# Part of the first expert's work moved into the routing of the last batch, and the router in half batches

## The chip, the cores and the metric

The kernel runs on one core of a Trainium2 chip. The core has TensorE (matmuls, PE in the profile; PEld is its weight load), VectorE (DVE), ScalarE (ACT), GpSimd (POOL) and SyncE (SP), which run side by side and wait for each other on semaphores, and DMA queues that SP and POOL fill. The metric is the device time of one execution in microseconds (us).

## The reference

In short, attention with a window, then a mixture of eight experts in which each token goes to one expert:

```python
scores = scale * np.matmul(q, k.transpose(0, 1, 3, 2)) + bias     # B 4, H 8, S 768, D 64
scores = np.where(is_global | is_local, scores, -1000000000.0)    # 8 global keys, 96 local
a = softmax(scores); x = (a @ v) -> (B*S, H*D) = (3072, 512)
logits = (x / |x|) @ (expert_emb / |expert_emb|).T / tau           # 8 experts
expert_idx = argmax(logits); gate_w = softmax(logits)[expert_idx]
for e in range(8):
    mask = expert_idx == e
    out[mask] = gate_w[mask, None] * (np.maximum(x[mask] @ w1[e], 0) @ w2[e])   # 512 -> 1024 -> 512
```

By the reference's own arithmetic the experts get 406, 310, 510, 319, 322, 369, 472 and 364 of the 3072 tokens; 315 of expert 0's are in the first three of the four batches.

## The kernel before

Everything is float32. `window_attention` runs 32 steps, four for each of eight groups (a batch has two groups of four heads). A step `s` of group `g` scores two units of 96 to 192 queries (`score`, L395), exponentiates them on ACT (`grow`, L399), multiplies them with a table on DVE (`weigh`, L406), transposes what later groups need (`turn`, L376), and multiplies the step before with v and with ones (`attend`, L421 and L429). After every second `attend` the three PSUM tiles `od` are copied to `xd` (ACT one, DVE two, L434 to L436); there is one set of `od`, so the next `attend` waits for these copies.

When a half batch has been attended to in both groups, its three chunks of 128 tokens are routed one chunk a step: `turn_x` transposes the attention output, `turn_sums` the softmax sums and the product of the chunk before (L456, L458), `store_x` scales a row, sends it to `x_dram` and squares it on ACT (L488), and `score_experts` multiplies with the expert embeddings (L494). `choose`, a generator in three parts, then finds the expert (DVE), ranks each token among those of its expert with two matmuls (L199 `prefix`, L200 `ones`) and a running count `cnt` (L213, L214, a pair for each chunk), and computes the gate. POOL scatters token number and gate to `meta`, one indirect DMA for each chunk (L228, `meta<-mt,slot`); `meta` has a list of slots for each expert.

The experts follow. `choose_widths` turns the counts into one of 13 widths for each expert, which each engine loads into a register (L836) for a switch. `load_rows` brings an expert's list (`emt<-meta`, on SP, after all scatters), converts it (`ids`, L753) and gathers the rows (`xg<-x_dram,ids`, POOL, four DMAs of 128 rows). `turn_rows` transposes them (L771), `expert` multiplies with `w1` in the width's arm (L809, 64 passes, a float32 matmul being two) and applies relu, and `second` multiplies with `w2`, 16 passes for each 128 slots (L781), scales, and scatters to the output (L785). While an expert computes, rows and weights (2 MB for `w1`, 2 MB for `w2`) of the next are loaded; those of expert 0 come in parts during attention.

PE, DVE, ACT and SP follow the order in which the code issues (`ORDERED`); POOL's order is found by the scheduler. An engine works strictly in its order.

## Time and profile before

| | us |
|---|---|
| median of 3 runs (lowest, highest) | 636.59 (631.88, 640.8) |
| the profiled execution's own time | 636.79 |
| its span in the profile | 634.8 |
| PE busy in the span | 559.0 (88%) |
| DVE busy | 169.8 |
| ACT busy | 141.6 |
| POOL busy | 99.6 |

The span starts with the first instruction that the profiler counts and ends with the last. Busy time is a sum over stages that have different limits, and a matmul that runs at half clock is busy twice as long.

### The profile page before, as it was taken

To read this page: it belongs to the slowest core of one execution; us is meant where nothing else is said; L and a number is where in the kernel's file an instruction comes from. 1 tells how busy PE (TensorE), PEld (TensorE's weight loads), DVE (VectorE), ACT (ScalarE), POOL (GpSimd) and SP (SyncE) were. 2 spreads that over 40 slices of the span, in tenths; PEclk is the share of its full clock that TensorE was granted. 3 is DMA by queue.
4 is the path that set the end of the run, shared out by engine and by line. 5 is a ranking of instruction groups with operands and counts; after the bars stand their busy time and mean duration, and the time that the engine had idled before them with its cause. 6 is when DMAs were issued, how large, how long until landed. Compare 5 with 4: busy or idle time off the path is not lost.

```text
span 634.8 us, 8682 instructions
## 1 busy us (share of the span) xinstructions
PE 559.0 (88%) x3314; PEld 338.6 (53%) x3314; DVE 169.8 (27%) x445; ACT 141.6 (22%) x345; POOL 99.6 (16%) x138
## 2 busy tenths in 40 slices
PE   4999998898596307999999999999999999999990
PEld 3778886686474204554744444655645544545540
DVE  2555667566375701021020020020100110100000
ACT  4866765665252100100100100100101101100100
POOL 2100004004003324001303001303013013011010
PEclk9999998998797556999999999999999999999995
DMA  9999899995002214722644113643346215010000
GB/s 184 214 208 252 212 233 129 65 230 131 34 18 67 36 15 123 265 89 88 217 152 161 68 50 138 218 153 116 119 160 218 101 69 217 2 36 34 1 34 22
DMA packets 109987, 77.40 MB, mean 122 GB/s; under 512 B 90744, under 2 KB 90872, under 8 KB 109826
## 3 DMA queue, kind: packets, MB, share of 16 engines
q1 hardware_dynamic: 100850, 60.16, 39.8%
q0 software_dynamic: 5488, 14.71, 6.4%
q10 hardware_dynamic: 3488, 0.79, 0.6%
q8 instruction: 52, 0.85, 0.6%
q14 instruction: 109, 0.89, 0.5%
HBM read 62.83 MB, written 13.59 MB: 120 GB/s over the span
## 4 chain that ended last, share of the span: by engine, by line
PE 59%; issue 2%; POOL 1%; DMA 1%; DVE 0%; POOLq 0%; DVEq 0%
PE work L781 29%; PE big L809 27%; PE work L771 2%; DMA xg<-x_dram,ids 1%; POOL xg L757 0%; POOL out_dram L785 0%; POOL meta L228 0%; DVE y L784 0%; POOLq L792 0%; DVE ids L753 0%; DVEq L993 0%; DVE flags L851 0%; DVE xT L772 0%; POOLq L757 0%
## 5 line engine op out<-in xcount | busy, mean ns | idle before, releaser
L781 PE MATMUL work<-w2t,hT 128*128 128x512 f32 x432 | 187.4, 594 | 0.0
L809 PE MATMUL big<-xT,w1t 128*128 128x320 f32 (+5 forms) x512 | 173.1, 499 | 2.6 <-issue 2.6
L809 PEld LDWEIGHTS big<-xT,w1t 128*128 128x128 f32 x512 | 97.9, 191 | 77.8 <-issue 45.0
L781 PEld LDWEIGHTS work<-w2t,hT 128*128 128x128 f32 x432 | 81.5, 190 | 101.0 <-issue 99.5
L811 ACT ACTIVATE hT<-big 128x640 f32<-128x640 f32 (+5 forms) x32 | 26.6, 830 | 355.8 <-PE big L809 355.8
L406 DVE TENSOR_TENSOR ex<-ex,table 126x768 f32<-126x768 f32 x64 | 57.9, 904 | 64.2 <-ACT ex L399 59.5
L785 POOL DMA_INDIRECT out_dram<-y,ids x27 | 26.9, 997 | 302.5 <-DVE y L784 230.5
L784 DVE TENSOR_SCALAR y<-work,emt 128x512 f32<-128x512 f32 x27 | 20.3, 751 | 185.2 <-PE work L781 185.2
L772 DVE COPY xT<-work 128x512 f32<-128x512 f32 x32 | 20.2, 685 | 159.3 <-PE work L771 159.3
L399 ACT ACTIVATE ex<-pa 126x384 f32<-126x384 f32 (+1 forms) x128 | 53.6, 476 | 30.3 <-PE pa L395 27.6
L395 PE MATMUL pa<-qT,kT 64*126 64x192 f32 (+1 forms) x512 | 50.6, 336 | 3.4 <-ACT qT L381 3.0
L421 PE MATMUL od<-ex,v 126*64 126x192 f32 (+1 forms) x576 | 47.8, 312 | 4.0 <-DVE xd L435 4.0
L395 PEld LDWEIGHTS pa<-qT,kT 64*126 64x126 f32 x512 | 41.4, 190 | 11.1 <-issue 5.9
L421 PEld LDWEIGHTS od<-ex,v 126*64 126x64 f32 x576 | 35.3, 139 | 12.5 <-DVE xd L435 4.5
L771 PE MATMUL work<-ident,xg 128*128 128x128 f32 x128 | 19.0, 295 | 22.5 <-DMA xg<-x_dram,ids 22.5
L228 POOL DMA_INDIRECT meta<-mt,slot x24 | 26.3, 1094 | 66.9 <-DVE ok L509 21.5
L757 POOL DMA_INDIRECT xg<-x_dram,ids x32 | 30.8, 962 | 25.3 <-issue 19.7
L771 PEld LDWEIGHTS work<-ident,xg 128*128 128x128 f32 x128 | 15.4, 151 | 27.4 <-issue 23.9
L429 PE MATMUL od<-ex,ones 126*32 126x192 f32 (+1 forms) x576 | 27.5, 315 | 0.0
L376 PE MATMUL pa<-ident,q 128*128 128x128 f32 x96 | 17.2, 297 | 7.8 <-ACT lS L497 7.2
L488 ACT ACTIVATE sq<-xs 128x512 f32<-128x512 f32 x24 | 15.1, 631 | 38.5 <-DVE xs L482 34.0
L376 PE MATMUL pa<-ident,k 128*128 128x128 f32 x96 | 17.2, 296 | 6.0 <-DMA k<-in_k_dram 5.5
(118 smaller groups left out, 286.5 us busy)
## 6 DMA issues: line engine op xcount, KB each, us to landing
w1t<-in_moe_w_dram SPq DMA_DIRECT2D x7, 2048.0 KB, 9.6
w2t<-in_moe_w_dram SPq DMA_DIRECT2D x7, 2048.0 KB, 12.5
v<-in_v_dram SPq DMA_DIRECT2D x32, 192.0 KB, 5.4
x_dram<-xs SPq DMA_DIRECT2D x24, 256.0 KB, 2.7
k<-in_k_dram SPq DMA_DIRECT2D x28, 192.0 KB, 4.4
q<-in_q_dram SPq DMA_DIRECT2D x28, 192.0 KB, 4.2
w1t<-in_moe_w_dram SPq DMA_DIRECT2D x4, 512.0 KB
w2t<-in_moe_w_dram SPq DMA_DIRECT2D x4, 512.0 KB, 5.1
```

The lines of the kernel that those rows point to most:

```text
L376: nc.tensor.transpose(ps[:, r * P : (r + 1) * P], src[:, 3 * half + r, :, :], k.ident[:])
L395: nc.tensor.matmul(u.sp[e][0:ROWS, a * n : (a + 1) * n], lhsT=t.kT[rows, j, 0:ROWS], rhs=t.qT[rows, j * BLK : j * BLK + n], start=True, st ...
L399: nc.scalar.activation(u.ex[:, e], u.sp[e][0:ROWS, 0 : 2 * u.n].rearrange("p (a c) -> p a c", a=2), AF.Exp, scale=k.scale)
L406: nc.vector.tensor_tensor(out=exv, in0=exv, in1=tab[:, :, 0 : u.n // BLK, :], op=ALU.mult)
L421: nc.tensor.matmul(g.od[a][e * D : (e + 1) * D, at : at + c1 - c0], lhsT=g.v[0:ROWS, 2 * a + e, u.j, :], rhs=u.ex[:, e, a, c0:c1], start=f ...
L429: nc.tensor.matmul(g.od[2][32 * i : 32 * i + 32, at : at + c1 - c0], lhsT=k.ones[0:ROWS, 0:32], rhs=u.ex[:, e, a, c0:c1], start=first, sto ...
L757: i = nc.gpsimd.indirect_dma_start(out=xg[:], out_offset=None, in_=k.x_dram[:], in_offset=bass.IndirectOffsetOnAxis(ap=ids[:, j : j + 1], ...
L771: k.nc.tensor.transpose(ps[:, c, :], xg[:, c * P : (c + 1) * P], k.ident[:])
L781: nc.tensor.matmul(ps[:], lhsT=hT[:, f, j * P : (j + 1) * P], rhs=w2[:, f, :], start=f == 0, stop=f == k.NF - 1)
L785: nc.gpsimd.indirect_dma_start(out=k.out[:, :], out_offset=bass.IndirectOffsetOnAxis(ap=ids[:, j : j + 1], axis=0), in_=y[:], in_offset=No ...
L809: nc.tensor.matmul(ps[:, i, 0:w], lhsT=w1[:, c, f * P : (f + 1) * P], rhs=xT[:, c, 0:w], start=c == 0, stop=c == k.NC - 1)
L811: nc.scalar.activation(hT[:, 2 * f2 : 2 * f2 + 2, 0:w], ps[:, :, 0:w], AF.Relu)
```

## The change

The softmax sums, products and scores of a half batch (three chunks) are now made at once: `turn_sums` is six matmuls against four columns of the identity in place of six transposes, `score_experts` four matmuls of 384 columns in place of twelve of 128. A half goes through phases 0 to 3, one a step. The router runs once for each of batches 0 and 1, and once for each half of batches 2 and 3. The rank's totals come from one matmul for each chunk that adds to the following chunks, so the loop of pairs on `cnt` is gone; the square root on POOL moves from the first part of `choose` to the second.

In the last batch the order of steps is: first halves of both groups, then second halves. After the third batch is routed (step 28) `first_base` notes how many of expert 0's slots are filled, up to 256, and `first_rows` (end of step 30) fetches the first 256 slots. `first_turn` transposes them ahead of the last `attend`. Their product with `w1` (`first_product`, eight pieces of 8 passes) stands in between and behind the routing of the last half, and their product with `w2` (`second`, twice) ahead of the remaining rows of expert 0, whose list now starts at a slot known at run time (a register of SP). The width of expert 0 is that of the remaining slots. The weights of expert 1 are loaded in the last four steps of attention, where they were loaded behind the rows of expert 1 before. `choose_widths` moves into the ordered part. `meta` has three numbers a slot: the row in `x_dram` (in which a zero row now lies between batches 2 and 3), the row of the output, and the gate. Pools wait tile by tile for the space that they take over.

TensorE, from the ranking of the last half batch on. Before (`lS` is a chunk's scores, `oh` the choice, `pi` the widths):

```order
L458 MATMUL pa<-ident,lS 128x128
L199 MATMUL pa<-oh,prefix 128x24
L200 MATMUL pa<-oh,ones 128x24
L494 MATMUL pa<-xd,enb 32x128 x4
L458 MATMUL pa<-ident,lS 128x128
L199 MATMUL pa<-oh,prefix 128x24
L200 MATMUL pa<-oh,ones 128x24
L836 TENSOR_LOAD pi
```

After (`xd` the attention output, `fxT` the first slots turned, `w1t` weights):

```order
L467 MATMUL pa<-ident,xd 128x4 x6
L477 MATMUL pa<-xd,enb 32x384 x4
L501 MATMUL pa<-ident,xd 128x128 x8
L574 MATMUL pa<-fxT,w1t 128x256 x4
L487 MATMUL pa<-ident,lS 128x128 x3
L574 MATMUL pa<-fxT,w1t 128x256 x4
L200 MATMUL pa<-oh,prefix 128x24
L203 MATMUL pa<-oh,ones 128x24
L203 MATMUL pa<-oh,ones 128x16
L203 MATMUL pa<-oh,ones 128x8
L574 MATMUL pa<-fxT,w1t 128x256 x24
L921 TENSOR_LOAD pi
```

The 64 passes of the first slots' product now stand around and behind the ranking, ahead of the register loads of `pi`.

SyncE, from the last stores of x on. Before (`emt` is the list of an expert's slots):

```order
L160 DMA w2t<-in_moe_w_dram 128x2x512
L486 DMA x_dram<-xs 128x512 x12
L747 DMA emt<-meta 128x4x2 x2
L993 UNCONDITIONAL_BRANCH
L144 DMA w1t<-in_moe_w_dram 128x4x1024
L149 DMA w2t<-in_moe_w_dram 128x8x512
```

After (`si` is the first slot at which the remaining ones start):

```order
L510 DMA x_dram<-xs 128x512 x6
L162 DMA w1t<-in_moe_w_dram 128x1024 x4
L1055 TENSOR_LOAD si
L1055 ISA x2
L510 DMA x_dram<-xs 128x512
L162 DMA w2t<-in_moe_w_dram 128x2x512 x2
L510 DMA x_dram<-xs 128x512
L831 DMA emt<-meta 128x2x3
L162 DMA w2t<-in_moe_w_dram 128x2x512 x2
L510 DMA x_dram<-xs 128x512 x4
L831 ISA
L831 DMA emt<-meta 128x4x3 x3
```

Expert 1's weights moved in eight parts ahead of and around the first list, and the four x stores of the last steps behind it.

GpSimd, from the scatters of the last batches on. Before (`ss` are the square sums):

```order
L228 DMA meta<-mt,slot 24576x2 x6
L182 TENSOR_TENSOR ss<-ss,half 128x3 x2
L226 COPY mt<-tokid 128x3
L228 DMA meta<-mt,slot 24576x2 x6
L757 DMA xg<-x_dram,ids 128x512 x4
```

After (`out_dram` is the kernel's output):

```order
L233 DMA meta<-mt,slot 28672x3 x3
L837 CAST ids<-emt 128x4
L841 DMA xg<-x_dram,ids 128x512 x2
L208 TENSOR_TENSOR ss<-ss,half 128x3
L231 COPY mt<-tok 128x3x2
L233 DMA meta<-mt,slot 28672x3 x3
L208 TENSOR_TENSOR ss<-ss,half 128x3
L233 DMA meta<-mt,slot 28672x3 x3
L921 TENSOR_LOAD pi x8
L841 DMA xg<-x_dram,ids 128x512 x4
L868 DMA out_dram<-y,ids 3072x512
```

The fetch of the first slots stands between the scatters of the third and the fourth batch, ahead of the root for the last batch's first half; eight register loads stand ahead of the gather of the remaining rows.

The core of the diff (the replaced loop over the steps, unused paths and constants are left out):

```diff
+FIRST = 256
...
-    nc.gpsimd.tensor_tensor(out=ss, in0=ss, in1=k.half[:, 0:n], op=ALU.pow)
...
     w = n * E
-    ohf = oh.rearrange("p t e -> p (t e)")
-    nc.tensor.matmul(cp[:, 0:w], lhsT=k.prefix[:], rhs=ohf, start=True, stop=True)
-    nc.tensor.matmul(cp[:, w : 2 * w], lhsT=k.ones[:], rhs=ohf, start=True, stop=True)
...
+    nc.tensor.matmul(cp[:, 0:w], lhsT=k.prefix[:], rhs=oh.rearrange("p t e -> p (t e)"), start=True, stop=True,
+                     skip_group_check=True)
+    for t in range(n):
+        nc.tensor.matmul(cp[:, (t + 1) * E : w + E], lhsT=k.ones[:],
+                         rhs=oh[:, t : t + 1, :].to_broadcast([P, n - t, E]), start=False, stop=True,
+                         skip_group_check=True)
+
+
+    nc.gpsimd.tensor_tensor(out=ss, in0=ss, in1=k.half[:, 0:n], op=ALU.pow)
     nc.vector.tensor_scalar_add(ss, ss, 1e-6)
...
-    both = new([2, n, E], "both")
-    nc.vector.tensor_copy(out=both.rearrange("p i t e -> p (i t e)"), in_=cp[:, 0 : 2 * w])
-    within, total = both[:, 0], both[:, 1]
-    for t in range(n):
-        nc.vector.tensor_tensor(out=within[:, t, :], in0=within[:, t, :], in1=k.cnt[:], op=ALU.add)
-        nc.vector.tensor_tensor(out=k.cnt[:], in0=k.cnt[:], in1=total[:, t, :], op=ALU.add)
+    both = new([n + 1, E], "both")
+    nc.vector.tensor_tensor(out=both, in0=cp[:, 0 : w + E].rearrange("p (t e) -> p t e", e=E),
+                            in1=k.cnt[:].unsqueeze(1).broadcast_to([P, n + 1, E]), op=ALU.add)
+    nc.vector.tensor_copy(out=k.cnt[:], in_=both[:, n, :])
+    within = both[:, 0:n, :]
...
-    nc.vector.scalar_tensor_tensor(out=slot, in0=best, scalar=float(k.N), in1=rank, op0=ALU.mult, op1=ALU.add)
+    nc.vector.scalar_tensor_tensor(out=slot, in0=best, scalar=float(k.SL), in1=rank, op0=ALU.mult, op1=ALU.add)
...
-    mt = new([n, 2], "mt")
-    nc.vector.reciprocal(out=mt[:, :, 1], in_=gate)
-    nc.gpsimd.tensor_copy(out=mt[:, :, 0], in_=k.tokid[:, b * k.NT + i0 : b * k.NT + i0 + n])
+    mt = new([n, 3], "mt")
+    nc.vector.reciprocal(out=mt[:, :, 2], in_=gate)
+    nc.gpsimd.tensor_copy(out=mt[:, :, 0:2], in_=k.tok[:, b * k.NT + i0 : b * k.NT + i0 + n, :])
...
-    def turn_sums(t, i):
-
+    def turn_sums(hf):
+
+        t, h = hf.t, hf.h
+        hf.ps = bank()
+        for c in range(3):
+            for m in range(2):
+                nc.tensor.matmul(hf.ps[:, 384 + (2 * c + m) * 4 : 384 + (2 * c + m + 1) * 4],
+                                 lhsT=t.groups[m].xd[h][:, 2, c * P : (c + 1) * P], rhs=k.ident[:, 0:P:32],
+                                 start=True, stop=True)
+        nc.vector.reciprocal(out=t.rd[:, 3 * h : 3 * h + 3, :],
+                             in_=hf.ps[:, 384:408].rearrange("p (c h) -> p c h", h=H))
+
+    def score_experts(hf, ps):
+
+        t, h = hf.t, hf.h
+        for a in range(4):
+            nc.tensor.matmul(ps[32 * a : 32 * a + 32, 0 : 3 * P], lhsT=k.enb[:, a, :],
+                             rhs=t.groups[a // 2].xd[h][:, a % 2, :], start=True, stop=True)
+        hf.lS = const.tile([P, 3 * P], F32, name="lS", tag="lS")
+        nc.scalar.copy(out=hf.lS[:], in_=ps[:, 0 : 3 * P])
...
+    def turn_products(hf):
+
+        t, h = hf.t, hf.h
...
+        for c in range(3):
+            nc.tensor.transpose(ps[:, c * P : (c + 1) * P], hf.lS[:, c * P : (c + 1) * P], k.ident[:])
+        tmp = const.tile([P, 12, 2, E], F32, name="lh", tag="lh")
...
+    def start_half(t, h):
+        hf = Net()
+        hf.t, hf.h, hf.phase = t, h, 0
+        late = t.b >= B - 2
+        hf.router = choose(k, t.b, 3 * h if late else 0, 3 if late else NT, t.lg, t.ss, rt_p) if late or h else None
+        return hf
...
+    def half_turns(hf):
+
+        t, i = hf.t, 3 * hf.h + hf.phase
+        xp = turn_x(t, i) if hf.phase < 3 else None
+        if hf.phase == 0:
+            turn_sums(hf)
+        elif hf.phase == 1:
+            turn_products(hf)
+        if xp is not None:
+            store_x(t, i, xp)
+        if hf.router:
+            if hf.phase == 1 or hf.phase == 3:
+                next(hf.router)
+            elif hf.phase == 2:
+                hf.router.send(bank())
+        if hf.phase == 3 and hf.h == 1:
+            check_sums(t)
...
+    def first_base():
+        k.base = k.const.tile([P, E], F32, name="base")
+        nc.vector.memset(k.base[:], 0.0)
+        nc.vector.tensor_scalar(out=k.base[:, 0:1], in0=k.cnt[:, 0:1], scalar1=float(FIRST), scalar2=None, op0=ALU.min)
+        k.si = k.const.tile([P, 1], I32, name="si")
+        nc.vector.tensor_copy(out=k.si[:], in_=k.base[:, 0:1])
+
+    def first_rows():
+        k.first = Net()
+        k.first.rows = load_rows(k, k.meta[0:FIRST, :], k.ea, k.ea2, FIRST // P, nc.gpsimd, k.ZR + 1)
+        k.first.xT = k.ea.tile([P, k.NC, FIRST], F32, name="fxT")
+        k.first.hT = k.ea.tile([P, k.NF, FIRST], F32, name="fhT")
+
+    def first_turn():
+        for j, xg in enumerate(k.first.rows[2]):
+            ps = bank()
+            for c in range(k.NC):
+                nc.tensor.transpose(ps[:, c * P : (c + 1) * P], xg[:, c * P : (c + 1) * P], k.ident[:])
+            nc.scalar.copy(out=k.first.xT[:, :, j * P : (j + 1) * P], in_=ps[:].rearrange("p (c n) -> p c n", c=k.NC))
+
+    def first_product(f):
+        if f % 2 == 0:
+            k.first.ps = bank()
+        ps = k.first.ps
+        for c in range(k.NC):
+            nc.tensor.matmul(ps[:, (f % 2) * FIRST : (f % 2 + 1) * FIRST], lhsT=k.w[0][0][:, c, f * P : (f + 1) * P],
+                             rhs=k.first.xT[:, c, :], start=c == 0, stop=c == k.NC - 1)
+        if f % 2:
+            nc.scalar.activation(k.first.hT[:, f - 1 : f + 1, :], ps[:].rearrange("p (i n) -> p i n", i=2), AF.Relu)
...
+    steps = [(g, p) for g in groups[: 2 * B - 2] for p in range(4)]
+    steps += [(g, p) for h in range(2) for g in groups[2 * B - 2 :] for p in (2 * h, 2 * h + 1)]
...
+        if s == len(steps) - 5:
+            early.close()
+            k.w.append(new_weights(k, k.second_weights()))
+        if s >= len(steps) - 4:
+            for i in range(2):
+                load_weights_part(k, 1, k.w[1], 2 * (s - len(steps) + 4) + i)
...
+        if waiting and (s >= 8 * (B - 1) or all(hf.phase >= 3 for hf in active)):
+            active.append(start_half(*waiting.pop(0)))
+        for hf in active:
+            half_turns(hf)
+            if (hf.t.b, hf.h, hf.phase) == (B - 2, 1, 3):
+                first_base()
...
+        if s == len(steps) - 2:
+            first_rows()
+        prev = t
+
+
+    first_turn()
+    for hf in active:
+        half_turns(hf)
+    attend(*steps[-1])
+    hf = start_half(t, 1)
+    xs = [turn_x(t, 3)]
+    turn_sums(hf)
+    score_experts(hf, bank())
+    xs += [turn_x(t, 4), turn_x(t, 5)]
+    store_x(t, 3, xs[0])
+    store_x(t, 4, xs[1])
+    first_product(0)
+    turn_products(hf)
+    next(hf.router)
+    store_x(t, 5, xs[2])
+    first_product(1)
+    hf.router.send(bank())
+    first_product(2)
+    next(hf.router)
+    check_sums(t)
+    for f in range(3, k.NF):
+        first_product(f)
...
+def load_rows(k, slots, gp, xgp, NJ=CAP // P, cast=None, upto=None):
...
+    mt = gp.tile([P, NJ, 3], F32, name="emt", tag="emt")
...
+    ids = gp.tile([P, NJ, 2], I32, name="ids", tag="ids")
+    (cast or nc.vector).tensor_copy(out=ids[:], in_=mt[:, :, 0:2])
...
+        nc.gpsimd.indirect_dma_start(
+            out=xg[:], out_offset=None, in_=k.x_dram[0 : upto or k.N + 1, :],
+            in_offset=bass.IndirectOffsetOnAxis(ap=ids[:, j, 0:1], axis=0),
...
+    k.need = k.const.tile([P, E], F32, name="need")
+    nc.vector.tensor_tensor(out=k.need[:], in0=k.cnt[:], in1=k.base[:], op=ALU.subtract)
...
         def prepare(e):
             t = Net()
             t.width = n.widths[e]
-            t.rows = load_rows(n, n.meta[e * n.N : e * n.N + CAP, :])
-            t.w = n.w[0]
-            if e > 0:
-                t.w = new_weights(n, (wp_a, wp_b)[e % 2])
-                load_weights(n, e, t.w, n.gathers if e == 1 else ())
+            at = e * n.SL
+            if e == 0:
+                at = nc.values_load(n.si[0:1, 0:1], engines=(SP,), min_val=0, max_val=FIRST)
+            t.rows = load_rows(n, n.meta[bass.ds(at, CAP), :], n.gp, n.xgp)
+            if e < 2:
+                t.w = n.w[e]
+            else:
+                t.w = new_weights(n, (wp_a, n.wp_b)[e % 2])
+                load_weights(n, e, t.w)
             return t
 
         with tc.manual_schedule(engines=ORDERED | set(ARMS)):
+            choose_widths(n)
             coming = prepare(0)
+            second(n, n.first.rows, n.first.hT, n.w[0][1], 0)
             hint(n, coming.width)
+            second(n, n.first.rows, n.first.hT, n.w[0][1], 1)
             coming.xT = n.xtp.tile([P, n.NC, CAP], F32, name="xT", tag="xT")
             turn_rows(n, coming.rows, coming.xT)
             for e in range(n.E):

```

## Rows read from the trace of the kernel before

**Rows 1.** The page, share of 40 slices: busy tenths of TensorE (PE).

```profile
PE   4999998898596307999999999999999999999990
```

**Rows 2.** Stretches: from:to in us, length, busy us (count) by engine, PEclk, DMA.

```profile
104.00:106.00 2.00, 2.00 (x24) 0.99 (x24) 1.73 (x3) 0.72 (x2) 1.70 (x2) 0.50 0.19 59
...
200.00:210.00 10.00, 7.53 (x49) 5.29 (x49) 4.62 (x19) 2.62 (x9) 5.68 (x6) 0.50 0.39 75
```

**Rows 3.** Timeline, attention's end to the first expert: start, us, engine, line, operation.

```profile
194.20 0.70 PE L429 MATMUL od<-ex,ones 126*32 126x192 f32 x16
...
211.81 0.48 PE L458 MATMUL pa<-ident,lS 128*128 128x128 f32 x1 [0.88 <-ACT lS L497]
...
220.16 0.18 DVE L225 RECIPROCAL mt<-gate 128x3 f32<-128x3 f32 x1
...
223.63 0.96 POOL L228 DMA_INDIRECT meta<-mt,slot  x1 [0.30 <-issue]
...
232.36 0.94 SPq L747 DMA_DIRECT2D emt<-meta  x2
...
234.42 0.17 DVE L753 CAST ids<-emt 128x4 int32<-128x4 f32 x1 [13.03 <-DMA emt<-meta]
...
238.90 1.09 PE L771 MATMUL work<-ident,xg 128*128 128x128 f32 x4 [21.30 <-DMA xg<-x_dram,ids]
...
243.39 1.08 PE L771 MATMUL work<-ident,xg 128*128 128x128 f32 x4 [0.45 <-DMA xg<-x_dram,ids]
```

**Rows 4.** The chain that ended last, by pieces: start, us, what.

```profile
247.08 24.05 PE big L809 x64
...
273.01 27.68 PE work L781 x64
...
300.69 17.23 PE big L809 x64
...
522.74 25.76 PE big L809 x64
```

**Rows 5.** Waits of TensorE before 250: who for whom, us, times, longest.

```profile
PE od L421 <- DVE xd L435: 4.0, 2, 2.0
```

**Rows 6.** Timeline of TensorE, two stalls inside attention.

```profile
102.48 2.12 PE L421 MATMUL od<-ex,v 126*64 126x192 f32 x16 [1.99 <-DVE xd L435]
...
167.95 0.90 PE L376 MATMUL pa<-ident,q 128*128 128x128 f32 x3 [7.18 <-ACT lS L497]
```

**Rows 7.** Timeline of TensorE, one routing step of batch 0 and the ranking matmuls.

```profile
88.77 0.32 PE L199 MATMUL pa<-oh,prefix 128*128 128x48 f32 x2
...
89.24 1.85 PE L421 MATMUL od<-ex,v 126*64 126x96 f32 x24
...
94.94 0.38 PE L456 MATMUL pa<-ident,xd 128*128 128x128 f32 x2
...
95.16 0.27 PE L458 MATMUL pa<-ident,lS 128*128 128x128 f32 x1
...
97.01 0.40 PE L494 MATMUL pa<-xd,enb 128*32 128x128 f32 x8
...
97.34 1.57 PE L395 MATMUL pa<-qT,kT 64*126 64x192 f32 x16
```

**Rows 8.** Timeline, square sums (ACT) and their root (POOL).

```profile
190.25 0.63 ACT L488 ACTIVATE sq<-xs 128x512 f32<-128x512 f32 x1 [2.13 <-DVE xs L482]
...
211.57 0.85 POOL L182 TENSOR_TENSOR ss<-ss,half 128x3 f32<-128x3 f32 x1 [4.38 <-ACT sq L488]
```

**Rows 9.** Line L836: TensorE's loads of the width indices into registers.

```profile
L836 PEldq TENSOR_LOAD <-pi x8: 297/302/498, 221.4 to 226.6; - x8
...
L836 PEldq SEQ_ASSERT  x8: 18/18/32, 222.3 to 227.2; - x8
```

**Rows 10.** DMA issues: tile, queue, count, KB each, median us to landing.

```profile
w1t<-in_moe_w_dram SPq DMA_DIRECT2D x7, 2048.0 KB, 9.6
...
w2t<-in_moe_w_dram SPq DMA_DIRECT2D x7, 2048.0 KB, 12.5
```

More of the change, by code (lines that the diff above doesn't have):

```diff
@@ new lines, in window_attention @@
+    for g in groups:
+        gi = groups.index(g)
+        pieces = [(g, a, i) for a in range(2) for i in (0, 2, 3, 1)]
+        at = [4 * gi - 4 + i // 2 for i in range(8)]
+        if gi == 0:
+            pieces, at = [(g, a, i) for i in (3, 1) for a in range(2)], [0, 0, 1, 1]
+        elif gi == 1:
+            at = [1, 1, 1, 2, 2, 2, 3, 3]
+        elif gi == len(groups) - 1:
+            pieces = [(g, a, i) for i in (0, 2, 3, 1) for a in range(2)]
+            at = [4 * gi - 4 + i for i in (0, 0, 0, 0, 1, 1, 2, 2)]
+        for s, x in zip(at, pieces):
+            turns[s].append(x)
@@ new lines, in window_attention @@
+    waiting, active = [], []
+    for s, (g, p) in enumerate(steps):
+        if s % 8 == 0:
+            pair = groups[s // 4 : s // 4 + 2]
+            t = new_batch(g.b)
+            t.groups = pair
+        ahead = s // 4 + 2
+        if ahead < len(groups):
+            if s % 4 == 0:
+                open_group(groups[ahead])
+            load_part(groups[ahead], s % 4)
+        if s % 2 == 1 and 9 <= s < 25:
+            load_weights_part(k, 0, k.w[0], (s - 9) // 2)
+        if s == len(steps) - 5:
+            early.close()
+            k.w.append(new_weights(k, k.second_weights()))
+        if s >= len(steps) - 4:
+            for i in range(2):
+                load_weights_part(k, 1, k.w[1], 2 * (s - len(steps) + 4) + i)
+        us = g.units[2 * p : 2 * p + 2]
+        for u in us:
+            score(u)
+        grow(us[0], 0)
+        grow(us[0], 1)
+        if s == 0:
+            next(table)
+        weigh(us[0])
+        grow(us[1], 0)
+        todo = [(x.pairs[a], i) for x, a, i in turns[s]]
+        if todo:
+            turn(*todo.pop(0))
+        grow(us[1], 1)
+        for x in todo:
+            turn(*x)
+        if s == 2:
+            next(table)
+        if 1 <= s <= 3:
+            emb.send(bank() if s == 3 else None)
+        if waiting and (s >= 8 * (B - 1) or all(hf.phase >= 3 for hf in active)):
[4 more added lines that the diff above has]
+                first_base()
+        weigh(us[1])
+        if s > 0:
+            q, qp = steps[s - 1]
+            attend(q, qp)
+            if q.m == 1 and qp % 2:
+                waiting.append((prev, qp // 2))
+        for hf in active:
+            if hf.phase == 0:
+                score_experts(hf, hf.ps)
+            hf.phase += 1
+        active = [hf for hf in active if hf.phase < (4 if hf.router else 3)]
+        if s == len(steps) - 2:
+            first_rows()
+        prev = t
```

269 lines of the change are left out of this document (88 added, 181 removed).

## The prediction, made before the changed kernel ran

> **What bounds the kernel now.** I read the slices of TensorE's busy time first [rows 1]: nearly full in the first quarter, a dip in the 11th slice, a hole from the 13th to the 16th (190 to 254 us), then full to the end. So the experts, from 247 us on, are a chain of matmuls with no gap [rows 4], and only fewer or faster passes could shorten it. What can be gained lies in front. The timeline says what the hole is [rows 3]: the last attend's ones end at 194.9, the last product of a chunk is turned at 211.8, the last gate is ready at 220.2, the third scatter is issued at 223.6, the list of slots is fetched at 232.4, and the first rows reach TensorE at 238.9 after a wait of 21.3 us. The first expert starts at 247.1 [rows 4]. From 194.9 to 247.1, 52.2 us, TensorE works little, and at the half level of its clock (0.50, 1.2 GHz) in the stretch that I read [rows 2]. Inside attention there are three more stalls: two of 2.0 us each behind the copies of `xd` on VectorE [rows 5, 6], and one of 7.2 us behind a copy on ScalarE [rows 6], for which I see no cause in the program. I leave that one in the sum.
>
> All below is set against the profiled execution: 636.79 us, of which 634.8 are span and 2.0 lie around it; the median of the runs is 636.59, the same.
>
> **What the moved work costs.** A pass costs 17.23/64 = 0.269 us in expert 1 (310 tokens, so width 320) and 25.76/64 = 0.4025 in expert 6 (472, width 480) [rows 4]; a straight line through both gives 0.216 at 256 and 0.136 at 160. Expert 0 (406 tokens, width 416) becomes 256 first slots, 64 x 0.216 = 13.8 us, and 150 remaining ones in width 160, 64 x 0.136 = 8.7 us; narrow passes could be held by their weight load, up to 12 us in all, which I keep for the range. Its four tiles of `w2` stay four at 27.68/4 = 6.9 us [rows 4]. So the passes grow by nothing worth a term, but 13.8 + 13.8 = 27.6 us of them leave the chain for the hole.
>
> **Term A, until the last attend ends** (194.9 before). A half batch's sums were three pairs of transposes, 0.22 us a pair (94.94 to 95.16) [rows 7], together 0.66; now 12 passes, each with a fresh load of 128 x 128 weights. The nearest rows are the ranking matmuls, four passes in 0.47 (88.77 to 89.24) [rows 7], 0.12 each: 1.4. Scores were three times 0.33 (97.01 to 97.34) [rows 7]; the same columns in a third of the passes cost between a third of that and all of it, and I take 0.7. With a little saved on the products a half costs 0.25 more (bounds -0.3 and +1), six halves 1.5. The rank's totals take 14 passes for batches 0 and 1 and two times 8 for batch 2 in place of 4 each, 32 passes more at 0.12: 3.8. The last batch's first half now stands wholly in front of the last attend: 4.7 us (three turns of x at 0.44, sums 1.4, scores 0.7, products 0.4, ranking 8 passes 0.95), of which one chunk, 1.2, stood there already: 3.5. The turn of the first slots, 8 transposes, 0.9. Sum of passes: +9.7.
>
> VectorE's third part of `choose` loses its twelve additions; they are what held back the copies of `xd` twice. I take both stalls as gone with the half clock that follows them (0.50 at 104 to 106 [rows 2]; I estimate 1.8 us lost each time): -2 x (2.0 + 1.8) = -7.6. What is late next is a new wait: the root now stands in the same part as its use, so VectorE waits in each ranking step for ScalarE's square and GpSimd's root, 0.63 + 0.85 and their hand-overs, some 2 us [rows 8], with `weigh` and then the copies of `xd` queued behind it and TensorE's next attend waiting for those. The step has about that much slack, since TensorE has more to do in it; bounds 0 and 2 us for each of five routers, I take 2 for all.
>
> The first slots' rows: step 28 routes the last of batch 2. From the gate to the first rows at TensorE it took 238.9 - 220.2 = 18.7 us [rows 3]. Adding 4.5 for `weigh` and the ranking on VectorE, the rows come 23 us after step 28 starts. TensorE gets to them after four steps, which I put at 4.0 + 6.3 + 4.9 + 5.4 = 20.6 from the passes above. It then waits 2 to 3 us, and the weights of expert 1, issued on the same queue around that list, may add one or so: 3.5, and 1.5 for the half clock behind it. Bounds 0 and 12. Behind SP's wait for these scatters stand two parts of `w2` and four stores of x, and since `xs` has two buffers now, a store held up would hold VectorE; but the list must be out before the first turn, and the stores behind it are made later, so I charge nothing (an SP held for longer is the second rival). SP's load of the start slot waits for VectorE in step 28 with one store behind it: nothing. GpSimd's root for the next half and with it VectorE's `weigh` stand behind that fetch too, but the last attend needs the turn of these rows first anyway.
>
> A ends at 194.9 + 9.7 - 7.6 + 2 + 5 = 204.0.
>
> The Trainium skill ("DMA: Bandwidth & Descriptors", section on the anatomy of one DMA) puts the fixed cost of a GpSimd DMA at about 2 us, most of it the write receipt. By that, scatter to list would cost some 6 us less, the first slots would be there in time, and the sum would be 5 us lower. The trace disagrees: from the end of the third scatter's issue, 224.6, to the list's issue at 232.4 it is 7.8 us [rows 3], and I go by the row.
>
> **Term B, from there to the first matmul of the remaining slots** (52.2 us before). Two paths. *Rows:* the last half is turned, scored, its products turned behind one piece of `first_product`, chosen and ranked; I get the last gate at 14 us (6.5 until the products are turned; then as in 211.8 to 220.2, 8.4 less what the other half took there, plus the new wait for the root). From gate to first matmul it was 247.1 - 220.2 = 26.9 [rows 3, 4]: 41. GpSimd's eight register loads stand ahead of the gather now, but inside the 7.8 us in which the scatters land. *TensorE's own:* turns 1.3, sums 1.4, scores 0.7, products 0.4, ranking 0.95, first product 13.8, waits in between 1.6 (estimate): 20.1. Then the eight loads of widths, which took 221.4 to 227.2, 5.8 us [rows 9], in the hole before, and now stand between the first slots' two products; with 0.9 of passes still queued ahead, 4.9 of idling: 25.0. Two tiles of `w2` 13.8, plus 2.2 for the half clock after the idling: 41.0. Sixteen transposes 1.8, and the branch into the width's arm 2.6 (244.5 to 247.1) [rows 3, 4]: **45.3**. TensorE's path is the later one and sets B, by 4 us.
>
> **Term C, the rest.** First product of 160: 8.7, plus 2.0 for a start at half clock (before: 24.05 - 64 x 0.349 = 1.7); transposes 1.8; two tiles 13.8: 26.3. Then from 300.7 to 634.8 as before, 334.1. Expert 1's rows are gathered while the remaining slots compute, and its weights are there; I see no wait. The rest of the diff (the fill of `meta` in more pieces, the zero row, the pools' finer waits, the start slot in the list's address, ScalarE's and VectorE's eight loads of widths, which end before the rows come) I put at nothing: it lies at the start, where SP has queues of loads ahead, or under the 7.8 us of landing. If that cover failed, each set of loads would cost up to 5.8 us on the rows' path, of which 4 are slack.
>
> **Sum:** 204.0 + 45.3 + 26.3 + 334.1 = 609.7 of span, and 2.0 around it: **612 us**, 25 less, 3.9%. In one line: 27.6 us of passes move into the hole, the hole's own end moves from 52.2 to 45.3 behind the attend (-7), and the attend ends 9 later.
>
> **The rivals.** *Heavier steps (within 2%).* If a narrow pass costs 0.19 in place of 0.12, the 136 of them in front of the last attend (seven halves' sums, 84, and 52 of the ranking) cost 9.5 us more, and with the full price of the new wait in each router, 4 to 8 more: 625 to 629. For it speaks that these passes load fresh weights each; against it, that four of them took 0.47.
>
> *The weights' queue (slower).* The 4 MB of expert 1, hidden under expert 0 before, are now issued by SP around the first list, on the same queue. Such loads of 2 MB landed after 9.6 and 12.5 us [rows 10]. If the list waits for all parts issued ahead of it and the rows then share the engines with the rest, TensorE stands at the first turn for up to 22 us more, and the pieces behind run at half clock, 27.6 us of them losing up to 13.8: 612 + 22 + 10 = 644. It decides from 25 us of added delay on. Against it: the parts go out from step 28 on, and the list only after step 30, when three quarters of them had some 15 us to land.
>
> *More than that.* If the 7.2 us stall on ScalarE and its half clock (9 us) were an accident of this execution and the first rows come in time (5): 598.
>
> *It does not do what it says.* With fewer than 256 slots filled at step 28, the remaining width would be larger; the reference has 315, so I give it nothing.
>
> **How the numbers follow.** 0.74 for the forecast's own range (600 to 624), 0.08 for below it, 0.13 for heavier steps or late rows within 2%, 0.05 for slower. The range 600 to 626 leaves out the accident and the queue. Faster by over 2% means below 623.9, about what a measurement here can tell from no change; faster 0.82, same 0.13, slower 0.05.
>
> **What would show it.** In the profile of the changed kernel: TensorE dense between attention and the experts, with two idle places, one ahead of the turn of `xg` before the last attend (3.5 us by me; over 12 is the queue's rival), and one of 5 us at the loads of `pi`; the last attend ending near 204; the first matmul of width 160 near 249; the stalls of attend behind `xd` gone. I am wrong if the first matmul comes after 262, or if attention alone ends after 215.

## The result, and the profile after

The change makes the kernel faster: 598.38 us (median; 595.75 to 599.17) against 634.24 (629.66 to 640.8), a ratio of 0.945 with a 95% interval of 0.9375 to 0.9525. The forecast was 612 with a range of 600 to 626: the right sign, and 14 us too little gain. The profiled execution took 598.26 us, of which 596.5 are span.

The page of the changed kernel, TensorE's busy tenths and granted clock in 40 slices. The hole of [rows 1] is gone, and the clock falls visibly only in two places.

```profile
PE   4989999999987989999999999999999999999990
...
PEclk9999999999989799999999999999999999999996
```

Its waits of TensorE (who for whom, us in total, times, longest) answer to [rows 5]. The wait of 21.3 us for the first rows [rows 3] and the one of 7.2 us behind ScalarE [rows 6] are not there; of the waits behind `xd` one of 2.2 is left.

```profile
PE pa L387 <- DMA k<-in_k_dram: 5.6, 2, 4.5
PE pa L566 <- DMA xg<-x_dram,ids: 3.3, 1, 3.3
...
PE pa L387 <- DMA q<-in_q_dram: 2.4, 1, 2.4
PE pa L501 <- DVE xd L446: 2.2, 1, 2.2
PE work L864 <- issue: 1.7, 1, 1.7
...
PE od L432 <- DVE ex L417: 0.5, 1, 0.5
```

TensorE's timeline around the last `attend` (L432, and L440 for its ones) shows the two places: passes that take up to twice as long behind each wait (24 passes of L432 take 3.36 us there, 1.85 elsewhere).

```profile
174.10 0.44 PE L501 MATMUL pa<-ident,xd 128*128 128x128 f32 x2 [2.19 <-DVE xd L446]
...
175.77 3.36 PE L432 MATMUL od<-ex,v 126*64 126x96 f32 x24
...
193.67 1.94 PE L566 MATMUL pa<-ident,xg 128*128 128x128 f32 x8 [3.26 <-DMA xg<-x_dram,ids]
195.54 2.19 PE L432 MATMUL od<-ex,v 126*64 126x192 f32 x16
197.65 1.19 PE L440 MATMUL od<-ex,ones 126*32 126x192 f32 x16
```

The chain that ended last, from there on (start, length, what), answers to [rows 4]: first product (L574), the first slots' second product (L864), and the remaining slots of width 160 from 236.96 on.

```profile
208.41 10.48 PE pa L574 x48
219.51 1.10 issue
220.61 13.99 PE work L864 x32
234.60 2.10 PE work L854 x16
236.96 8.93 PE big L892 x64
245.89 1.93 PE work L854 x16
247.85 13.97 PE work L864 x32
261.82 17.23 PE big L892 x64
```

Against the forecast's terms:

| | before | forecast | after | off by |
|---|---|---|---|---|
| A: the last attend ends at | 194.9 | 204.0 | 198.8 | -5.2 |
| B: from there to the first matmul of the remaining slots | 52.2 | 45.3 | 38.1 | -7.2 |
| C: from there to expert 1 | 53.6 | 26.3 | 24.9 | -1.4 |
| expert 1 to the end | 334.1 | 334.1 | 334.7 | +0.6 |

A is called the head below, the rest of the span the tail. The next table has both for the profiled execution of every kernel; the median is of its runs. A kernel's runs mostly agree within 1.5%, but kernels were measured on several chips of the same kind, and a letter marks those that were measured one after the other on one chip. There the kernel before took 640.4 (a), 636.9 (b), 634.5 (c) and 637.2 us (d), by the median of those runs that lie within 1.5% of its fastest.

| kernel | median | span | head | tail |
|---|---|---|---|---|
| before | 634.24 | 634.8 | 194.9 | 439.9 |
| before once more (a) | 639.1 | 638.1 | 197.6 | 440.5 |
| before, rows of 3 numbers (b) | 619.84 | 618.5 | 182.9 | 435.6 |
| before, rows of 4 numbers (c) | 616.69 | 614.7 | 183.1 | 431.6 |
| before, lists further apart (b) | 629.97 | 631.0 | 190.3 | 440.7 |
| changed | 598.38 | 596.5 | 198.8 | 397.7 |
| changed once more (c) | 596.8 | 594.8 | 196.8 | 398.0 |
| changed, rows of 2 numbers (c) | 599.12 | 597.5 | 199.6 | 397.9 |
| changed without first slots (a) | 624.89 | 626.4 | 198.8 | 427.6 |
| start slot behind `xd` (a) | 598.91 | 597.4 | 199.7 | 397.7 |
| list ahead of a store (a) | 598.49 | 596.7 | 198.9 | 397.8 |
| list ahead of store and weights (b) | 609.06 | 606.6 | 208.6 | 398.0 |
| the same once more (c) | 591.52 | 589.8 | 191.8 | 398.0 |
| first slots' products left out (b) | 613.99 | 613.3 | 216.1 | 397.2 |
| list ahead, widths fixed (d) | 605.87 | 603.5 | 208.9 | 394.6 |

### The profile page after: what moved, and what is told of

Read it like the earlier page. It is cut to its first block, busy times and chain, and to the rows that moved or that the text cites. A ratio compares the mean times of both kernels' runs of the same rounds, so it can differ in the third digit from the quotient of the medians.

```text
span 596.5 us, 8717 instructions
## 1 busy us (share of the span) xinstructions
PE 560.2 (94%) x3346; PEld 351.2 (59%) x3346; DVE 162.0 (27%) x375; ACT 141.7 (24%) x336; POOL 100.7 (17%) x146
## 4 chain that ended last, share of the span: by engine, by line
PE 78%; issue 8%; DMA 3%; POOL 3%; DVE 2%; ACT 2%; SPq 0%; ACTq 0%; DVEq 0%; POOLq 0%
PE work L864 31%; PE big L892 26%; PE pa L406 4%; PE od L432 4%; PE work L854 3%; PE pa L387 3%; DMA q<-in_q_dram 2%; PE od L440 2%; POOL meta L233 2%; PE pa L574 2%; PE pa L467 1%; PE pa L501 1%; DMA xg<-x_dram,ids 1%; ACT ex L410 1%; DVE ex L417 1%
## 5 line engine op out<-in xcount | busy, mean ns | idle before, releaser
L864 PE MATMUL work<-w2t,hT 128*128 128x512 f32 x400 | 173.7, 594 | 0.0
L892 PE MATMUL big<-xT,w1t 128*128 128x320 f32 (+5 forms) x512 | 158.0, 469 | 0.3 <-issue 0.3
L892 PEld LDWEIGHTS big<-xT,w1t 128*128 128x128 f32 x512 | 93.8, 190 | 64.6 <-issue 31.8
L864 PEld LDWEIGHTS work<-w2t,hT 128*128 128x128 f32 x400 | 75.4, 190 | 93.4 <-issue 92.1
L894 ACT ACTIVATE hT<-big 128x640 f32<-128x640 f32 (+5 forms) x32 | 24.9, 777 | 316.3 <-PE big L892 316.3
L432 PE MATMUL od<-ex,v 126*64 126x192 f32 (+1 forms) x576 | 48.9, 316 | 0.5 <-DVE ex L417 0.5
L432 PEld LDWEIGHTS od<-ex,v 126*64 126x64 f32 x576 | 36.1, 142 | 8.2 <-issue 2.9
L841 POOL DMA_INDIRECT xg<-x_dram,ids x34 | 32.8, 965 | 18.7 <-issue 11.1
L233 POOL DMA_INDIRECT meta<-mt,slot x24 | 24.9, 1039 | 33.1 <-DVE good L527 8.6
L440 PE MATMUL od<-ex,ones 126*32 126x192 f32 (+1 forms) x576 | 26.8, 310 | 0.0
L208 POOL TENSOR_TENSOR ss<-ss,half 128x3 f32<-128x3 f32 (+1 forms) x6 | 6.3, 1048 | 105.2 <-ACT junk L511 105.2
L511 ACT ACTIVATE junk<-xs 128x512 f32<-128x512 f32 x24 | 15.2, 631 | 32.9 <-DVE xs L506 28.9
L440 PEld LDWEIGHTS od<-ex,ones 126*32 126x32 f32 x576 | 15.0, 111 | 9.0 <-issue 3.5
```

The costliest lines, as they stand in the source:

```text
L233: i = nc.gpsimd.indirect_dma_start(out=k.meta[:], out_offset=bass.IndirectOffsetOnAxis(ap=slot[:, t : t + 1], axis=0), in_=mt[:, t, :], in ...
L432: nc.tensor.matmul(g.od[a][e * D : (e + 1) * D, at : at + c1 - c0], lhsT=g.v[0:ROWS, 2 * a + e, u.j, :], rhs=u.ex[:, e, a, c0:c1], start=f ...
L440: nc.tensor.matmul(g.od[2][32 * i : 32 * i + 32, at : at + c1 - c0], lhsT=k.ones[0:ROWS, 0:32], rhs=u.ex[:, e, a, c0:c1], start=first, sto ...
L841: nc.gpsimd.indirect_dma_start(out=xg[:], out_offset=None, in_=k.x_dram[0 : upto or k.N + 1, :], in_offset=bass.IndirectOffsetOnAxis(ap=id ...
L864: nc.tensor.matmul(ps[:], lhsT=hT[:, f, j * P : (j + 1) * P], rhs=w2[:, f, :], start=f == 0, stop=f == k.NF - 1)
L892: nc.tensor.matmul(ps[:, i, 0:w], lhsT=w1[:, c, f * P : (f + 1) * P], rhs=xT[:, c, 0:w], start=c == 0, stop=c == k.NC - 1)
```

## The experiments

**Is the 7.2 us stall an accident?** The kernel before, unedited.

> The kernel before, once more. If the 7.2 us in which all engines stood (160.8 to 167.9, named as ScalarE's copy of lS) were an accident of that one execution, it is absent here or at another place, the last attend ends near 186 (9 us earlier, the stall and its half clock) and the time is 627 to 630. If the program causes it, a stall of 6 to 8 us stands at the same copy and the time is 634 to 639.

639.1 us, ratio to the kernel before 0.999 (0.994 to 1.004). The stall of [rows 6] is absent, and the time no better: TensorE stood elsewhere in the same part, as its timeline shows.

```profile
116.44 0.72 PE L477 MATMUL pa<-ident,xd 128*128 128x128 f32 x4 [2.58 <-issue]
129.06 0.69 PE L477 MATMUL pa<-ident,xd 128*128 128x128 f32 x2 [4.54 <-issue]
```

Both readings that I had offered fall. What the two profiles of the kernel before have in common is the DMA behind batch 0's six scatters to `meta` (101 to 109 us). The DMA issues of 100 to 112 in this execution (tile, queue, count, KB each, median us to landing):

```profile
v<-in_v_dram SPq DMA_DIRECT2D x3, 192.0 KB, 20.7
x_dram<-xs SPq DMA_DIRECT2D x2, 256.0 KB, 22.2
...
meta<-mt,slot POOLq DMA_INDIRECT x6, 20.4
```

and of the changed kernel in 84 to 100, where its six scatters stand:

```profile
v<-in_v_dram SPq DMA_DIRECT2D x4, 192.0 KB, 5.4
...
meta<-mt,slot POOLq DMA_INDIRECT x6, 6.4
```

The loads of v beside the scatters land four times later in the kernel before. I call this the jam.

**What makes the jam?** Two edits of the kernel before, one for the size of a list row (three numbers in `mt`, `meta`, its fill and `emt`), one for the distance between the experts' lists (e x 3072 rows to e x 3584).

```diff
-    mt = new([n, 2], "mt")
+    mt = new([n, 3], "mt")
+    nc.gpsimd.tensor_copy(out=mt[:, :, 2], in_=k.tokid[...])
```

> The kernel before with rows of three numbers (12 bytes) in the list of slots, not two (8 bytes); the third is a copy of the first. In both profiles of the kernel before the six scatters of batch 0 took some 20 us to land, loads of v issued beside them 17 to 22 us (4 to 5.5 elsewhere), and TensorE stood here and there for 2 to 7 us; in the changed kernel the same six took 6.4 us. Theory 1, the size of a row does it: the jam and the stalls are gone, 625 to 629. Theory 2, something else does it (how far apart the experts' parts of the list are, or when the router runs): 634 to 640 as before.

> The kernel before with the experts' parts of the list 3,584 slots apart (28,672 bytes), not 3,072 (24,576 bytes); rows stay 8 bytes. Theory 1, the distance decides: scatters land in some 6 us, no jam, 625 to 629. Theory 2, the size of a row: the jam stays, 634 to 640.

Rows of three numbers: 619.84 us, ratio 0.972 (0.962 to 0.982). Lists further apart: 629.97, 0.986 (0.981 to 0.991), with one stall of 4.5 us left behind batch 0's scatters and none at batch 1's: its head is 190.3 for 197.6 and 194.9, so neither theory holds in full. Four numbers, 16 bytes, on another chip:

> The kernel before with list rows of four numbers (16 bytes). With rows of three it took 619.8, with two 634 to 647. Theory 1, the larger the row the less the scatters jam: 615 to 621. Theory 2, the gain of the wider row was a chance of where the list lay: anywhere up to 640.

616.69, ratio 0.971 (0.967 to 0.976). The stretch behind batch 0's scatters (from:to, length, PEclk, DMA share, GB/s) in the kernel before, second profile, with rows of three, and with rows of four:

```profile
105.00:115.00 10.00, 0.92 1.48 43
```

```profile
105.00:115.00 10.00, 0.91 1.07 105
```

```profile
105.00:115.00 10.00, 0.88 1.12 120
```

With 8-byte rows the engines are busier (1.48 for 1.07 and 1.12) and move less than half of the bytes; what the time goes to, the trace does not say. The waits of TensorE with rows of four have no stall of 7.2 us or of "issue" any more; what is left is the old list of [rows 5]:

```profile
PE work L772 <- DMA xg<-x_dram,ids: 17.4, 3, 15.1
...
PE pa L495 <- DVE lh L467: 4.8, 3, 4.0
PE pa L199 <- DVE ss L203: 4.3, 1, 4.3
PE od L422 <- DVE xd L436: 4.0, 2, 2.0
```

So the size of a row in `meta`, which the change raised from two numbers to three so that the first slots could be addressed, is worth some 18 us in the kernel before (both ratios): 12 in the head, 4 to 8 in the tail. My reading of the diff had no term for it. A wider row also sets the lists further apart in bytes (36,864 and 49,152 for 24,576), and 28,672 with rows of 8 bytes took a part of the jam away; size and distance are not fully told apart. The converse, rows of two in the changed kernel:

> The changed kernel with list rows of two numbers (8 bytes), as in the kernel before; where a row goes in the output is worked out from its token's number by four small operations of VectorE. Theory 1, the size of a row makes the jam behind the scatters: landings of 10 to 20 us and stalls of TensorE come back in batches 0 and 1, 606 to 618. Theory 2, it was the moment at which the router runs, or the distance between experts: 596 to 600.

599.12, against 596.8 for the changed kernel on that chip: 2.3 us, not 10 to 20. The jam is back, but shorter: the six scatters land after 11.5 us, and the stretch behind them reads

```profile
100.00:105.00 5.00, 1.00 1.77 74
```

yet TensorE waits for nothing there. So wider rows are enough to free the kernel before, and the changed kernel would be nearly free without them. Which other part of it does that is open: the lists lie further apart, which alone left the kernel before at 630, and the router runs about 13 us earlier, which was not tried alone.

**What are the first slots worth?** The changed kernel without them (`first_rows`, `first_turn`, `first_product` and their `second` taken out, the list of expert 0 from slot 0).

> The changed kernel without the first slots: all 406 tokens of expert 0 go through it after the routing, only the router by half batches is left (and expert 1's weights early). My theory, that the overlap is worth most: the last attend ends near 193 (198.8 less the wait for rows, their turn and the half clock behind it), the first matmul of width 416 comes 39 later, the first expert takes 54 as before: 620 to 624. Rival, that the finer router gave most of the gain: below 610.

624.89, as the first theory had it: with the first slots some 26 us less (598.4 to 598.9). The chain of the kernel without them, from the first expert to the second:

```profile
237.34 25.40 PE big L886 x64
...
292.30 17.23 PE big L886 x64
```

Between the two lie 55.0 us, with the first slots 24.9. The hole's end stands where it did, 38.6 us behind the attend for 38.1, so the moved passes cost the hole nothing. The heads look equal (198.8) by accident only: in the profile of the kernel without first slots k and q came late near 37 us, and it enters step 28 5.1 us behind the other.

```profile
36.17 0.52 PE L387 MATMUL pa<-ident,k 128*128 128x128 f32 x3 [1.25 <-DMA k<-in_k_dram]
38.95 0.87 PE L387 MATMUL pa<-ident,q 128*128 128x128 f32 x3 [2.27 <-DMA q<-in_q_dram]
```

So the first slots take some 30 us from the tail (427.6 to 397.7) and give about 5 back in the head, where their rows are waited for and turned. The finer router by itself gains nothing against a kernel before without the jam (616.7 and 619.8); it costs 5 to 8 us: the tail shrinks by 4 to 8, and the head grows from 183 to some 194.

**The path of the rows alone.** The products of the first slots left out.

> Leaves out both products of the first slots (their rows of the output are not written), so that only the path of the remaining rows is left behind the last attend. In the changed kernel TensorE's path gave 38.1 us from the last attend to the first matmul of width 160. Theory 1 (my forecast: rows 4 us ahead of TensorE): 34 to 37 us, and 594 to 598 with the slower start at half clock. Theory 2, TensorE's own passes are the whole bound: 25 to 30 us, below 592.

Theory 1 holds for the path, not for the time. TensorE's timeline, from the last ones of attend (end 216.1) to the first matmul of width 160:

```profile
214.91 1.19 PE L440 MATMUL od<-ex,ones 126*32 126x192 f32 x16
...
242.18 1.08 PE L849 MATMUL work<-ident,xg 128*128 128x128 f32 x4 [18.36 <-DMA xg<-x_dram,ids]
...
251.37 4.07 PE L887 MATMUL big<-xT,w1t 128*128 128x160 f32 x14 [2.85 <-issue]
```

35.3 us, against 38.1 with the products: they cost 2.8. Its time of 614 comes from its head, 17 us longer than the changed kernel's, of which more below.

**The two waits of the head.** First the start slot behind the copies of `xd`, in the same step 28:

```diff
-            if (hf.t.b, hf.h, hf.phase) == (B - 2, 1, 3):
-                first_base()
         weigh(us[1])
...
             attend(q, qp)
+            if any((hf.t.b, hf.h, hf.phase) == (B - 2, 1, 3) for hf in active):
+                first_base()
```

> The three small operations that work out the start slot stand behind VectorE's two copies of xd in step 28, not ahead of them. Theory 1: the wait of 2.2 us of TensorE at 172 shrinks to 1.5 or less and the half clock behind it (175.8 to 178.9) goes, and the later steps follow: 2 to 4 us less, 594 to 596. Theory 2: the first slots' rows come when they did (193.7), so TensorE only waits longer for them: 598, no change.

598.91: no change (from step 28's first turn of x to the end of the last attend 27.2 us for 27.4). The wait went from 2.2 to 1.8 us only, since the third part of `choose` and the test of the sums still stand ahead of the copies; the next wait, for the first rows, is 3.5 for 3.3.

Then the first slots' list. SP fetched it at 185.7 in the changed kernel, though the scatters were out at 176.2: ahead of it in SP's order stands a store of x that was ready at 185.0.

> SP fetches the first slots' list ahead of the store of x in step 30, not behind it. Theory 1: the list was held until 185.7 by that store, which waits for VectorE at 185.0; now it goes when the scatters have landed, 4 us after the last one's issue, near 180.5; the rows come 5 us earlier, TensorE's wait of 3.3 us for them and the half clock behind it go: 5 us less, 593. Theory 2: the scatters need 7.8 us to land, as in the kernel before: the list goes at 184, 1.7 us earlier: 596.5.

598.49. The list left 5.5 us earlier and arrived late, as the timeline shows (SP's issue, and GpSimd's conversion that waits for it):

```profile
178.91 0.97 SPq L162 DMA_DIRECT2D w2t<-in_moe_w_dram  x2
180.20 0.37 SPq L831 DMA_DIRECT2D emt<-meta  x1
...
186.75 0.19 POOL L837 CAST ids<-emt 128x4 int32<-128x4 f32 x1 [8.98 <-DMA emt<-meta]
```

It took 6.5 us behind 1 MB of expert 1's weights on the same queue. In the changed kernel it took 2.4. TensorE's wait for the rows fell from 3.3 to 2.4 us, and the stretch from step 28's first turn to the last attend by 1.5; the time hides this, since late loads near 37 us cost this execution 1.5 us more than the other. So ahead of those weights too:

```diff
+        if s == len(steps) - 2:
+            first_rows()
         if s >= len(steps) - 4:
             for i in range(2):
                 load_weights_part(k, 1, k.w[1], ...)
```

> The changed kernel with the first slots' list fetched ahead of the two parts of w2 of step 30 as well as of the store of x. With the store alone moved behind it the list left SP 5.5 us earlier but landed after 6.5 us, not 2.4. Theory 1, it queued behind those 1 MB: now it lands in some 2.5 us, the rows come 4 to 5 us earlier than in the changed kernel, TensorE waits for them 0 to 0.5 us (3.3 before) and the half clock behind goes: 593 to 594. Theory 2, any transfer beside those of the weights takes that long: 597 to 598.

609.06, and no theory holds: the wait for the first rows is gone, but the head is 208.6. A stall of 3.7 us stands at 94 and one of 2.3 at 145 to 148, long ahead of the edit. So the changed kernel and this one were measured together on another chip:

> The changed kernel once more, unedited. Two kernels that differ from it only late in the program (the first slots' list ahead of the weights; the first slots' products left out) lost 8 to 9 us near 94 us and 4 to 8 us near 148 us, each time just behind six scatters, where their instructions are the changed kernel's. Theory 1, the stalls hang on how a kernel happens to lie or start and can meet any of these kernels: this one may come out anywhere from 596 to 612, the same in all its rounds. Theory 2, they hang on those edits: 596 to 599 again.

> The kernel with the first slots' list ahead of step 30's weights, once more, unedited (609 the first time, the last attend ending at 213). Theory 1 (chance of the loading): without the stalls near 94 and 148 us it comes out at 593 to 597. Theory 2 (the edit): 607 to 611 again with the stalls at the same places.

596.8 and 591.52 us. The move is worth 5.3 us, and the ratio of 0.932 (0.928 to 0.935) to the kernel before makes it the best version found. Its first slots' rows:

```profile
176.06 0.38 SPq L831 DMA_DIRECT2D emt<-meta  x1
176.50 1.01 SPq L162 DMA_DIRECT2D w2t<-in_moe_w_dram  x2
180.88 0.96 POOL L837 CAST ids<-emt 128x4 int32<-128x4 f32 x1 [6.47 <-DMA emt<-meta]
...
188.55 1.32 PE L566 MATMUL pa<-ident,xg 128*128 128x128 f32 x8
```

TensorE no longer waits for them. The list still took 4.8 us, with the weights issued behind it; in the first measurement of the same kernel it took 1.9 (192.4 to 194.3). How much of the 6.5 us the weights ahead of it made is thus not settled.

What the disturbed profile shows at 94 us is that VectorE and ScalarE wait for nothing that the trace knows ("remote"), and TensorE for them:

```profile
97.70 0.56 DVE L447 COPY xd<-od 128x384 f32<-128x384 f32 x1 [4.06 <-remote]
97.77 1.10 ACT L410 ACTIVATE ex<-pa 126x384 f32<-126x384 f32 x3 [3.93 <-remote]
...
98.31 0.55 PE L387 MATMUL pa<-ident,k 128*128 128x128 f32 x3 [3.65 <-ACT ex L410]
```

The same stalls, at the six scatters of batch 0 and at those of batch 1, stand in the two other kernels with a long head (products left out, widths fixed), and in no kernel of the chips a and c that has the change. Each of these three heads is some 17 us longer than that of its like without the stalls (208.6 and 208.9 for 191.8, 216.1 for 198.8); 12 to 16 of them are lost at these two places, with the half clock behind them, and up to 3.5 to late loads near 37 us. They look like the stall of [rows 6]; what they wait for is not settled.

**The loads of widths and the branch.** The list ahead as above, the widths written in:

```diff
-        v = nc.values_load(pi[0:1, e : e + 1], engines=ARMS, ...)
...
+    k.widths = [WIDTHS.index(w) for w in (160, 320, 512, 320, 352, 384, 480, 384)]
```

> The changed kernel with the first slots' list ahead of the weights and the store of step 30 (591.5 when undisturbed), and with the widths written into the program (160, 320, 512, 320, 352, 384, 480, 384): it leaves out the choice of the widths at run time, the eight loads on every engine and the branches. Theory 1: the loads cost TensorE only the 1.7 us that it stands in the changed kernel, and the branches some 0.3 each: 588 to 590.5, with no wait between the first slots' two products, and the first matmul of width 160 35 to 37 us behind the last attend. Theory 2 (as forecast, 4.9 us of loads, 2.2 of half clock behind them and 2.6 of a branch, of which a part is hidden in some other place): 582 to 586.

605.87 us, with the long head; the tail, which the stalls don't touch, is 394.6 against 398.0. That is 3.4 less, as theory 1 has it. TensorE's timeline from the last ones of attend (end 208.9) on has no wait at the loads and none at the branch:

```profile
218.00 10.61 PE L574 MATMUL pa<-fxT,w1t 128*128 128x256 f32 x48
228.44 13.90 PE L864 MATMUL work<-w2t,fhT 128*128 128x512 f32 x32
242.17 2.26 PE L854 MATMUL work<-ident,xg 128*128 128x128 f32 x16
244.38 5.84 PE L892 MATMUL big<-xT,w1t 128*128 128x160 f32 x41
```

From 208.9 to 244.4 it is 35.5 us, against 38.1: 2.6 less. What the loads cost at another place, and how the gain goes with the number of first slots, was not measured.

## Where the prediction was right, and where it failed

**Right: what is moved and what it is worth.** 27.6 us of passes were to leave the chain for the hole; against the run without first slots the first expert's part shrinks by 30.1, of which some 3 are the start at half clock, and the hole grows by nothing. "TensorE's path is the later one and sets B, by 4 us": by 2.8. The 136 narrow passes cost what I took (a half's sums 12 passes in 1.4 us), so the rival of heavier steps falls. Turns, sums, scores, products, ranking and first product with their waits were put at 20.1 us; they took 20.0 (198.84 to 218.87, where L574 ends). The second product was put at 13.8 and took 14.0.

**Failed: "I leave that one in the sum."** The stall of 7.2 us and its half clock were not the program's price for attention but one place of the jam, and the rest of the jam was left in with it. Without the jam the kernel before has a head of 183, so 12 of its 194.9 us go. This is the largest single error; the other terms of A hid 6.8 of it, so that A missed by 5.2 only. The rival that I gave 0.08 for 598 named the stall, but as "an accident of this execution" and with first rows that come in time; neither is so, and that 598 came out is luck. Stalls stand in both profiles of the kernel before, at changing places, and the rows were waited for 3.3 us.

From 183, the head grew by 13.7 to 15.9 (196.8 and 198.8), and I had 9.1. Passes: +9.7 forecast; TensorE is busy 9.9 us longer in the head than before (181.1 for 171.2), and 12.2 longer than with rows of four (169.0). All of these hold passes at half clock, so the term fits in size but is not shown by itself. The wait for the first rows: 3.5 forecast, 3.3 measured, with some 2.6 of half clock behind it for 1.5. The root: 2 forecast, 0.5 measured. The old stalls behind `xd` went, as forecast (-7.6), but a new one of 2.2 came in step 28, with some 1.6 of half clock: what I took from `choose` there, the start slot and the test of the sums put back. That is 3.8 that the sum did not have. In the first profile a late q adds 2.4.

**Failed: the price of the loads in B.** "With 0.9 of passes still queued ahead, 4.9 of idling", "plus 2.2 for the half clock", and 2.6 for the branch: 9.7 us. TensorE stood 1.7 and 0.3, 2.0 in all, and its clock stayed at 1.00 from 200 us on. The rows of the loads in the changed kernel (duration min/median/max, first and last start):

```profile
L921 PEldq TENSOR_LOAD <-pi x8: 296/300/487, 214.8 to 219.9; - x8
```

They begin at 214.8, when the passes that end at 218.87 had been issued: 4.1 us, 19 passes of 0.22, were queued, not 0.9 us. I had read 5.8 us of loads [rows 9] in a place where TensorE had nothing queued, and kept the price for a place where it had. The Trainium skill ("TensorE: Matmul & The Clock Gate", section on the array of 16 small ones, its paragraph on queue depths) gives TensorE a queue of 64 instructions; 19 passes with their weight loads are 38, which agrees, though no run here shows the limit. These three terms were 7.7 us too high; the passes and turns of B took 0.5 more than I had, which leaves the miss of 7.2.

**C** lost 1.4 since no half clock is left to start from (8.9 for 8.7 + 2.0).

**The weights' queue** (644, 0.05) cost the changed kernel nothing that shows: its list took 2.4 us. Moved ahead of the store alone, it took 6.5 behind the weights, far from the 22 of the rival.

**Scatter to list.** I took 7.8 us between the third scatter's end and the list's issue from [rows 3] and set it against the 2 us that the Trainium skill gives ("DMA: Bandwidth & Descriptors", section on the anatomy of one DMA). With rows of four numbers it is 1.5 (211.0 to 212.5), with three 4.2 (211.0 to 215.2), in the changed kernel 4.0 (216.3 to 220.3). So that row, too, held some of the jam. It decided nothing, since TensorE's path was the later one.

## What to carry to other kernels

A stall for which the program has no cause is not a constant of the kernel: ask what else was in flight at each of its places, and give the case that it goes a price and a chance of its own, above all when the change touches the transfers around it. A cost read where an engine was idle (register loads, a branch) must be set anew where the engine has a queue of passes ahead. Small DMAs that wait in an ordered queue are late by what stands ahead of them there, a store that is not ready or a megabyte of weights, and both have to be moved.

## What was not expected of the hardware

Six scatters of 128 rows of 8 bytes slowed everything on the DMA engines for some 20 us: loads of v took 20.7 us for 5.4, at a busy share of 1.48 and 43 GB/s. Rows of 12 and 16 bytes moved 105 and 120 GB/s in that stretch, and the kernel took 619.8 and 616.7 us for 634 to 640. In the changed kernel six scatters of 8-byte rows landed after 11.5 us for 6.6 and cost 2.3 us, so it is not the size alone; what else it hangs on stays open. The Trainium skill ("DMA: Bandwidth & Descriptors", section "Specifications") says that transfers under 512 bytes are done as read, change and write; that puts all three sizes on the same side. The runs tell 8 bytes from 12 by some 18 us, so the rule alone doesn't explain it.

A kernel's time can differ by 17 us between two chips at the same code (609.06 and 591.52), with stalls behind the scatters on the one, where VectorE, ScalarE and TensorE stood, and none on the other. Each kernel was measured once on a chip, so whether the chip or the way the program came to lie there makes it is not shown. Differences of a few us are safe only between kernels that ran on one chip, or part by part, as the tails above, which agree within 0.8 us over eight profiles of the changed kernel and its kin with run-time widths. In the heads, loads of k and q that came late near 37 us alone made up to 7 us of difference.
